# Stage four of a mixed-radix Fourier transform in quarters of the array, one pool of eight PSUM banks, and shorter rows

## The chip, the cores and the metric

The kernel runs on one NeuronCore of a Trainium2 chip. The metric is the device time in microseconds (us) of one launch, lower is better; the median of several runs counts. The engines are named as the profile names them: PE (TensorE, matmuls; PEld its weight loads), DVE (VectorE), ACT (ScalarE), POOL (GpSimd), SP (SyncE, which here only issues DMAs).

## The reference, cut to what matters

Eight sequences of 2496 tokens with 256 features are filtered along the sequence in frequency, and each token of the result then goes through one of eight experts.

```
X = np.fft.rfft(x, axis=1)                       # x: (8, 2496, 256)
Y = X * (filt_r + 1j * filt_i)[None]
y = np.fft.irfft(Y, n=2496, axis=1)
x = y.reshape(19968, 256)
logits = x @ w_gate                              # 8 experts
e = argmax(logits);  gate = softmax(logits)[e]
out = gate * (relu(x @ w1[e]) @ w2[e])           # w1: 256x1024, w2: 1024x256
```

Everything is in fp32.

## The kernel before, in words

**The transform.** 2496 is 39 x 64, so the transform over a sequence is one over 39 points (index q) for each of 64 residues t, and one over 64 points. A sequence goes through four stages, each a product with a table that lies in SBUF as the stationary operand.

- Stage one, `stage_a` (line 530): three residues t at a time, 3 x 39 = 117 rows by table `tas` give 3 x 2 x 20 = 120 rows (20 cosine and 20 sine coefficients for each residue; TP = 117, TK = 120, NB = 3). A residue group is a slot, there are NG = 22 of them, the last with one residue only. A chunk (`CH`) is four slots, or two at the end: 5 chunks of four and one of two in a batch.
- Stage two, `stage_b` (line 543): the 64-point transform on 128 rows, and the filter, four VectorE operations for each product.
- Stage three, `stage_c` (line 565): the 64-point transform back.
- Stage four, `stage_d` (line 580): back from 120 coefficients to 117 tokens with table `tds`. For each two slots of a chunk there is one product of 120 x 128 by 512 columns into a PSUM bank, which `evac` (line 410) copies to the tile `yo` on VectorE or ScalarE, whichever the planner has free first. In the last chunk the two slots have 120 and 40 rows and are two products of 256 columns.

Between stages one and two, and between three and four, a batch is written to DRAM (`zd`, `ud`) and read back in the other order; `by_part` (line 503) and `columns` (line 473) give the two orders. Batch 0 stays in SBUF instead (`first_a`, `turn_z`, `first_c`, `turn_u`).

**The routing.** `turn_y`, `block_logits` and `block_back` (lines 671 to 710) compute the logits of a chunk; from batch 3 on (`by_blocks`, line 690) the transpose is VectorE's. The logits' products go to 32 columns of the array each, four beside each other, into a PSUM bank of their own (`psr`, lines 697 and 718). `route` (line 739) finds the expert and the place of each token, writes the token's number and its gate into eight words each behind the 256 features of `yo` (rows of DR = 272 words, line 341), and scatters the rows to `rowsd` in DRAM, one indirect DMA on POOL for a slot, 22 a batch.

**The experts.** `rows_in` (line 949) reads the sorted rows of a tile of 512 (or 256, or 128) tokens; `hidden_by_quarters` (line 1020) and `hidden` compute the first product, `result` (line 1083) and, late in the kernel, `result_by_quarters` (line 1146) the second. The forms by quarters make seven block products out of eight, with sums on VectorE and POOL; that of the second product needs sums of the weights from POOL (`w2_sums`), and begins when the transforms are over (`late`).

**The order.** One loop at the end of the kernel writes all instructions. It plays the engines' clocks in a model (`Order`, line 125, with a cost for each instruction) and picks, step by step, either a transform step of the list that `slot` (line 1217) makes, or a step of one of the two streams of expert products; a step may be taken when its inputs and a PSUM bank (two for steps over 0.9 us of TensorE) are free in the model (`wait_of`). Each step is a tuple of due time, function, input it needs loaded, TensorE time by the model, stream, and what must be ready. Slot k holds stages two and three of batch k, stage one of batch k + 1 and stage four of batch k - 1. SBUF loads go out on SP in the order of the steps (`more_loads`), stores when their data is ready in the model (`move`, `flush`). PSUM has seven banks in one pool (line 354), of which `bank` (line 396) takes the one free first, and the eighth for the logits (line 359).

Of the kernel before, what the change touches and what calls it, by code (L numbers as in the profile page):

```python
# [19 lines left out]
P = 128  # L20
# [14 lines left out]
TK = NB * NS  # L35
DH = D // P
# [4 lines left out]
NJ = D // CT  # L41

# [13 lines left out]
def dft_tables():  # L56

    w = 2.0 * np.pi
    q = np.arange(N1)
    t = np.arange(N2)

    ta = np.zeros((NB, N1, NB, NS))
    td = np.zeros((NB, NS, NB, N1))
    for f in range(NF):
        ang = w * ((q * f) % N1) / N1
        for j in range(NB):  # L70
            ta[j, :, j, f] = np.cos(ang)
            td[j, f, j] = (2.0 if f else 1.0) / S * np.cos(ang)
            if f:
                ta[j, :, j, NF + f] = -np.sin(ang)
                td[j, NF + f, j] = -2.0 / S * np.sin(ang)

    ang = w * ((t[:, None] * t[None, :]) % N2) / N2
    c, sn = np.cos(ang), np.sin(ang)
    tb = np.block([[c, -sn], [sn, c]]).reshape(2, N2, P).transpose(1, 0, 2).reshape(P, P)
    tc = np.block([[c, sn], [-sn, c]]).reshape(P, 2, N2).transpose(0, 2, 1).reshape(P, P)  # L80

    ids = np.zeros((NB, N1, NG))
    valid = np.zeros((NB, N1, NG))
    for j in range(NB):
        for i in range(len(range(j, N2, NB))):
            ids[j, :, i] = token(q, NB * i + j)
            valid[j, :, i] = 1.0

    by_block = np.zeros((4, CT, NG + 2))
    by_block.reshape(P, NG + 2)[:TP, :NG] = valid.reshape(TP, NG)  # L90
    by_block = by_block.reshape(4, CT, -1, 4).transpose(3, 1, 2, 0).reshape(P, -1)

    sg = np.where(coefficients() <= S // 2, 1.0, -1.0)

    return {
        "ta": ta.reshape(TP, TK),
        "tb": tb,
        "tc": tc,
        "td": np.pad(td.reshape(TK, TP), ((0, 0), (0, P - TP))),
        "sg": np.concatenate([sg[:, :NF // 2], sg[:, NF // 2:]]),  # L100
        "ids": ids.reshape(TP, NG),
        "valid": np.concatenate([np.pad(valid.reshape(TP, NG), ((0, P - TP), (0, 0))), by_block], axis=1),
    }


def lay_x(x):

    out = np.zeros((x.shape[0], P, NG, D), x.dtype)
    q = np.arange(N1)
    for j in range(NB):  # L110
        for i in range(len(range(j, N2, NB))):
            out[:, j * N1:(j + 1) * N1, i] = x[:, token(q, NB * i + j)]
    return out
# [11 lines left out]
class Order:  # L125
# [53 lines left out]
    def count(self, engine, op, args, named):  # L179
# [31 lines left out]
        else:  # L211
            if out is None:
                took = 0.8 if engine == "sync" else 0.02
            elif engine == "tensor":
                if start > self.busy + 1.2:
                    self.slow = start + 3.4
                rows = out.ap[0][1]
                took = max(0.1, 0.00085 * n) if op == "transpose" else max(0.216, 0.00169 * n) if rows > 32 else 0.00045 * n
                took *= 2.0 if start < self.slow else 1.0
                tail = 0.25  # L220
            elif engine == "vector":
                took = 0.15 + n / 960
            elif engine == "scalar":
                took = 0.16 + n / 1200
            else:
                took = 0.2 + n / 480
# [24 lines left out]
class Slots:  # L251
# [3 lines left out]
    def freed(self, name, tag):  # L255

        if name is None:
            return 0.0
        if tag in self.live and name in self.live[tag]():
            return 1e9  # L260
        return max(self.order.done.get(name, 0.0), self.order.used.get(name, 0.0)) + 0.1
# [32 lines left out]
def kernel(  # L294
# [12 lines left out]
    ids: bass.AP,  # L307
    valid: bass.AP,
# [25 lines left out]
    TR = E * TE  # L334

    dram = open_pool(ctx, name="dram", bufs=1, space=DRAM)
    zd = [dram.tile([N2, NS, D], F32, tag=f"z{b % 2}", name="zd") for b in range(B)]
    ud = [dram.tile([N2, NS, D], F32, tag=f"u{b % 2}", name="ud") for b in range(B)]


    DR = D + 16
    rowsd = dram.tile([TR, DR], F32, tag="rows", name="rows")
# [11 lines left out]
    ps = open_pool(ctx, name="ps", bufs=7, space=PSUM)  # L354
# [4 lines left out]
    psr = open_pool(fft, name="psr", bufs=1, space=PSUM)  # L359

    tas = cst.tile([TP, TK], F32, name="tas")
    tbs = cst.tile([P, P], F32, name="tbs")
    tcs = cst.tile([P, P], F32, name="tcs")
    tds = cst.tile([TK, P], F32, name="tds")
# [15 lines left out]
    ids0 = cst.tile([TP, NG], F32, name="ids0")  # L380
    vld = cst.tile([P, 2 * NG + 2], F32, name="vld")
# [12 lines left out]
    ps.live["bank"] = lambda: ()  # L394
# [25 lines left out]
    def load_filters(c):  # L420
        f0, n = FH[c]
        if c == 0:
            nc.sync.dma_start(out=tbs, in_=tb)
# [11 lines left out]
        if c == 0:  # L435
            nc.sync.dma_start(out=tcs, in_=tcm)

    def load_rest():
        nc.sync.dma_start(out=tds, in_=td)
# [33 lines left out]
    def columns(ap, i0, n):  # L473

        rows = ap.rearrange("t s d -> (t s) d")
        m = min(n, NG - 1 - i0)
        yield TK, slice(0, m), rows[i0 * TK:(i0 + m) * TK, :].rearrange("(i p) d -> p i d", p=TK)
        if m < n:
            yield NS, slice(m, n), rows[(NG - 1) * TK:, :].rearrange("(i p) d -> p i d", p=NS)
# [23 lines left out]
    def by_part(ap):  # L503

        return ap.rearrange("t (c f) d -> (t c) f d", c=2)

# [8 lines left out]
    def load_z(b, c):  # L515
        f0, n = FH[c]
        zi = fin(("z", b, c))
        nc.sync.dma_start(out=zi[:, :n], in_=by_part(zd[b])[:, f0:f0 + n, :])

    def load_u(b, c):  # L520
        i0, n = CH[c]
        ui = fin(("u", b, c))
        for r, m, v in columns(ud[b], i0, n):
# [5 lines left out]

    def stage_a(b, c):  # L530
        i0, n = CH[c]
        xt = ins.pop(("x", b, c))
        zo = sb.tile([TK, 4, D], F32, tag="st", name="zo", bufs=4)
        for j in range(0, n, 2):
            p = bank()
            mm(p[:TK, :], lhsT=tas, rhs=xt[:TP, j:j + 2, :], start=True, stop=True)
            evac(zo[:, j:j + 2, :], p[:TK, :].rearrange("p (t d) -> p t d", t=2), 512)
        for r, m, v in columns(zd[b], i0, n):
# [4 lines left out]
    def stage_b(b, f):  # L543
# [6 lines left out]
        mm(p, lhsT=tbs, rhs=zi[:, j:j + 2, :], start=True, stop=True)  # L550
# [14 lines left out]
    def stage_c(b, f):  # L565
# [4 lines left out]
        uo = outs["u", b]  # L570
        p = bank()
        mm(p, lhsT=tcs, rhs=ys, start=True, stop=True)
        evac(uo[:, j:j + 2, :], p.rearrange("p (i d) -> p i d", i=2), 512)
        if j == 2:
            f0 = f - 2
            move(by_part(ud[b])[:, f0:f0 + 4, :], uo)
# [3 lines left out]
    def stage_d(b, c):  # L580
# [7 lines left out]
        yo = outs["o", b, c] = sb.tile([P, 4, DR], F32, tag="y", name="yo", bufs=YB)  # L588
        for j in range(0, n, 2):
            p = bank()  # L590
            if i0 + j + 2 < NG:
                mm(p, lhsT=tds, rhs=ui[:TK, j:j + 2, :], start=True, stop=True)
# [6 lines left out]


# [12 lines left out]
    def first_a(c):  # L613
        i0, n = CH[c]
        xt = ins.pop(("x", 0, c))
        for j in range(0, n, 2):
            p = bank()[:, :4 * TK]
            for h in range(DH):
                for i in range(2):
                    mm(p[:, (2 * h + i) * TK:(2 * h + i + 1) * TK], lhsT=xt[:TP, j + i, h * P:(h + 1) * P], rhs=tas,  # L620
# [21 lines left out]
    def first_c(f):  # L642
        ys = outs.pop(("y", 0, f))
        p = bank().rearrange("p (h i t c) -> p h i t c", h=DH, c=2, i=2)
        for i in range(2):
            for h in range(DH):
                mm(p[:, h, i].rearrange("p t c -> p (t c)"), lhsT=ys[:, i, h * P:(h + 1) * P],
                   rhs=tcs, start=True, stop=True)
# [44 lines left out]
    def block_logits(b, c):  # L693
# [3 lines left out]
        lt = psr.tile([P, 2, E * NG], F32, tag="lt", name="lt").rearrange("p i w -> p (i w)")[:, :n * CT]  # L697
# [14 lines left out]
    def logits(b, g):  # L712
# [5 lines left out]
        lt = psr.tile([P, 2, E * NG], F32, tag="lt", name="lt")[:, :, :TP]  # L718
# [20 lines left out]
    def route(b, c0, c1):  # L739
# [63 lines left out]
        if by_blocks(b):  # L803
# [13 lines left out]
            nc.vector.tensor_copy(row.rearrange("p (c g) -> p g c", g=4), pr[:, :, 0])  # L817
# [5 lines left out]
        for i, yo in enumerate(yos):  # L823
            n = min(4, w - 4 * i)
            sh8 = (TP, n, 8)
            nc.gpsimd.tensor_scalar(
                yo.bitcast(I32)[:TP, :n, D:D + 8], in0=ids0[:, t0 + 4 * i:t0 + 4 * i + n, None].to_broadcast(sh8),
# [3 lines left out]
        for i in range(w):  # L831
            m = N1 if t0 + i == NG - 1 else TP
            rows.append((row[:m, i:i + 1], yos[i // 4][:m, i % 4, :]))
        for i, (at, what) in enumerate(rows):
            m = what.ap[0][1]
            nc.gpsimd.tensor_copy(what[:, D + 8:], sd[:m, i:i + 1].to_broadcast((m, 8)))
# [7 lines left out]
    def pad_rows():  # L844
# [7 lines left out]
        nc.gpsimd.memset(fill.bitcast(I32)[:, D:D + 8], N)  # L852
# [96 lines left out]
    def rows_in(i):  # L949
# [4 lines left out]
        ng = gis[i] = pools["moe"].tile([P, 4, DR - D], F32, tag="ng", name="ng", bufs=8)  # L954
# [128 lines left out]
    def result(i, j):  # L1083
# [12 lines left out]
        gate = gis[i][:, j, 8:9]  # L1096
# [49 lines left out]
    def result_by_quarters(i):  # L1146
# [7 lines left out]
        gate = gis[i][:, :, 8:9]  # L1154
# [62 lines left out]
    def slot(k):  # L1217
# [12 lines left out]
        elif k < B:  # L1230
            for f in range(0, NF + 4, 2):
                at = f / (NF + 4)
                if f < NF:
                    steps.append((at, lambda f=f: stage_b(k, f), ("z", k, f // 4) if f % 4 == 0 else None, 0.85, "b", lambda f=f: count("y") < 4 and [ins["z", k, f // 4]]))
                if f >= 4:
                    steps.append((at + 0.01, lambda f=f: stage_c(k, f - 4), None, 0.85, "c", lambda f=f: [outs["y", k, f - 4], 0.0 if f % 4 else sb.free("st") - 0.9]))
        if k + 1 < B:
            for c in range(nch):
                steps.append(((0.25 if k == 0 else 0.0) + 0.7 * c / nch, lambda c=c: stage_a(k + 1, c), ("x", k + 1, c), 0.43 * CH[c][1], "a", lambda c=c: [ins["x", k + 1, c], sb.free("st") - 0.9]))
        if k > 0:  # L1240
            for c in range(nch + 3):
# [3 lines left out]
                if c < nch:  # L1245
                    steps.append((at, lambda c=c: stage_d(k - 1, c), ("u", k - 1, c) if k > 1 else "y", 0.43 * CH[c][1], "d",
                                  lambda c=c: [ins["u", k - 1, c] if k > 1 else outs["ui", c], sb.free("y") - 0.9]))
                if by_blocks(k - 1):
                    if 1 <= c <= nch:
                        steps.append((at + 0.03, lambda c=c: turn_y(k - 1, c - 1), None, 0.0, "d", lambda c=c: len(yts) < 2 and [outs["o", k - 1, c - 1]]))  # L1250
# [174 lines left out]
    def second_products():  # L1425

        for i in range(NT - RARE):
            if late and i < LARGE:
# [37 lines left out]
    with tc.manual_schedule(engines=None):  # L1466
        warm()
        nc.sync.dma_start(out=tas, in_=ta)
# [5 lines left out]
        def wait_of(f):  # L1474
# [11 lines left out]
            banks = ps.free("bank") if f[3] < 0.9 else max(ps.free("bank"), ps.free("bank", 1) - 0.85)  # L1486
# [15 lines left out]
        while fs or any(heads):  # L1502
# [7 lines left out]
            choice[0 if credit > 0.0 or not fs else 1:0] = products  # L1510
# [64 lines left out]
```

## Time and profile before

| what | us |
|---|---|
| median of three runs | 1476.66 (1476.07 to 1478.16) |
| the profiled execution | 1478.19 |
| its span on the core | 1476.5 |
| PE busy, records | 1440.1, 7828 |
| weight loads busy | 1147.0 |
| DVE busy | 848.7 |
| POOL busy | 822.0 |
| ACT busy | 480.6 |
| stage four of batch 3 begins, of batch 7 ends | 282, 879 |
| last scatter of rows begins | 959.8 |

A busy time is the sum of the times in which the engine had at least one instruction under way; matmuls overlap each other, so a record's mean length is longer than the time that it adds. A product in fp32 shows as two matmul records. The time before 970 us holds the transforms with expert products between them; what follows is expert products alone.

### The profile page before, as it was taken

To read this page: it belongs to the slowest core of one execution; us is meant where nothing else is said; L and a number is where in the kernel's file an instruction comes from. 1 tells how busy PE (TensorE), PEld (TensorE's weight loads), DVE (VectorE), ACT (ScalarE), POOL (GpSimd) and SP (SyncE) were. 2 spreads that over 40 slices of the span, in tenths; PEclk is the share of its full clock that TensorE was granted. 3 is DMA by queue.
4 is the path that set the end of the run, shared out by engine and by line. 5 is a ranking of instruction groups with operands and counts; after the bars stand their busy time and mean duration, and the time that the engine had idled before them with its cause. 6 is when DMAs were issued, how large, how long until landed. Compare 5 with 4: busy or idle time off the path is not lost.

```text
span 1476.5 us, 25693 instructions
## 1 busy us (share of the span) xinstructions
PE 1440.1 (98%) x7828; PEld 1147.0 (78%) x7828; DVE 848.7 (57%) x1819; ACT 480.6 (33%) x1004; POOL 822.0 (56%) x1213
## 2 busy tenths in 40 slices
PE   8998998999999999999999999999999999999998
PEld 6543656877677777776787778879999998999997
DVE  4667579235866675457665465567878775431110
ACT  4554452333332232322222232223232322223332
POOL 4434445635555654655465656858989878831111
PEclk9999999999999999999999999999999999999999
DMA  9759889795985585556544735556655425456661
GB/s 269 230 193 340 280 291 299 253 258 185 321 206 167 172 260 151 131 162 229 156 119 132 214 93 148 153 177 188 173 173 167 133 71 137 135 189 176 174 190 43
DMA packets 216383, 278.19 MB, mean 188 GB/s; under 512 B 124131, under 2 KB 163708, under 8 KB 216245
## 3 DMA queue, kind: packets, MB, share of 16 engines
q1 hardware_dynamic: 197125, 233.19, 53.2%
q0 software_dynamic: 19120, 43.33, 8.4%
q8 instruction: 66, 1.08, 0.3%
q14 instruction: 72, 0.59, 0.1%
HBM read 196.45 MB, written 80.64 MB: 188 GB/s over the span
## 4 chain that ended last, share of the span: by engine, by line
PE 85%; DVE 6%; DMA 4%; issue 3%; ACT 1%; POOL 0%; SPq 0%; DVEq 0%; POOLq 0%; ACTq 0%
PE bank L246 83%; DMA fin<-in_x_dram 2%; PE lt L246 2%; DVE hT L246 1%; DVE yw L246 1%; DVE ys L246 1%; DMA fin<-ud 1%; DMA fin<-zd 1%; DMA zd<-zo 1%; POOL out_dram L246 0%; DVE take L246 0%; ACT hT L246 0%; SPq L246 0%; DMA w1t<-in_moe_w_dram 0%; DMA xg<-rows 0%
## 5 line engine op out<-in xcount | busy, mean ns | idle before, releaser
L246 DVE TENSOR_TENSOR hT<-bank,hT 128x512 f32<-128x512 f32 (+1 forms) x504 | 301.9, 626 | 181.4 <-PE bank L246 101.2
L246 PE MATMUL bank<-w2t,hT 128*128 128x256 f32 (+1 forms) x1984 | 388.6, 350 | 1.6 <-DVE hT L246 1.6
L246 PEld LDWEIGHTS bank<-w2t,hT 128*128 128x128 f32 x1984 | 334.5, 190 | 49.9 <-issue 9.6
L246 PE MATMUL bank<-xT,w1t 128*128 128x256 f32 (+1 forms) x1728 | 314.9, 328 | 0.3 <-DVE hT L246 0.3
L246 POOL DMA_INDIRECT out_dram<-ys,ng x161 | 160.0, 994 | 252.5 <-ACT ys L246 121.5
L246 PEld LDWEIGHTS bank<-xT,w1t 128*128 128x128 f32 x1728 | 264.6, 191 | 33.1 <-issue 9.9
L246 ACT ACTIVATE hT<-hT 128x1024 f32<-128x1024 f32 (+1 forms) x144 | 135.5, 960 | 399.8 <-DVE hT L246 387.4
L246 POOL DMA_INDIRECT rows<-yo,row x176 | 181.9, 1033 | 70.8 <-POOL yo L246 31.3
L246 ACT ACTIVATE ys<-bank,ng 128x256 f32<-128x256 f32 x102 | 48.4, 475 | 287.4 <-PE bank L246 231.7
L246 PE MATMUL bank<-sums,wsum 128*128 128x256 f32 (+1 forms) x576 | 135.7, 358 | 1.5 <-DVE hT L246 1.5
L246 PE MATMUL bank<-w2s,hT 128*128 x592 | 132.9, 380 | 1.3 <-ACT hT L246 1.3
L246 POOL TENSOR_TENSOR wsum<-w1t 128x256 f32<-128x256 f32 x72 | 60.1, 835 | 114.5 <-PE bank L246 96.7
L246 PEld LDWEIGHTS bank<-w2s,hT 128*128 128x128 f32 x592 | 110.2, 190 | 15.8 <-ACT hT L246 2.0
L246 PEld LDWEIGHTS bank<-sums,wsum 128*128 128x128 f32 x576 | 100.3, 190 | 21.6 <-issue 11.3
L246 DVE STREAM_TRANSPOSE xT<-xg 128x512 f32<-128x512 f32 (+2 forms) x126 | 57.5, 494 | 57.7 <-PE bank L246 56.9
L246 PE MATMUL bank<-ys,tcs 128*128 128x512 f32 x140 | 73.8, 613 | 7.6 <-DVE yw L246 4.2
L246 DVE TENSOR_TENSOR ys<-bank,ht 128x512 f32<-128x512 f32 x80 | 54.9, 686 | 44.3 <-PE bank L246 38.0
L246 PE MATMUL bank<-fin,tds 120*128 120x512 f32 (+1 forms) x168 | 77.1, 580 | 3.1 <-DMA fin<-ud 2.6
L246 PE MATMUL bank<-fin,tas 117*120 117x512 f32 x154 | 75.5, 608 | 4.2 <-DMA fin<-in_x_dram 3.3
L246 PE MATMUL bank<-fin,tbs 128*128 128x512 f32 x140 | 72.7, 607 | 2.3 <-DMA fin<-zd 2.2
L246 ACT ACTIVATE hT<-bank 128x128 f32<-128x128 f32 (+1 forms) x191 | 57.2, 303 | 53.9 <-PE bank L246 45.3
L246 PE MATMUL bank<-xT,wsum 128*128 128x256 f32 (+1 forms) x288 | 68.8, 362 | 1.1 <-DVE yw L246 0.9
(171 smaller groups left out, 1778.9 us busy)
## 6 DMA issues: line engine op xcount, KB each, us to landing
w1t<-in_moe_w_dram SPq DMA_DIRECT2D x126, 512.0 KB
w2t<-in_moe_w_dram SPq DMA_DIRECT2D x68, 512.0 KB
fin<-in_x_dram SPq DMA_DIRECT2D x39, 512.0 KB
fin<-zd SPq DMA_DIRECT2D x35, 512.0 KB
ud<-uo SPq DMA_DIRECT2D x35, 512.0 KB
fin<-ud SPq DMA_DIRECT2D x35, 512.0 KB
zd<-zo SPq DMA_DIRECT2D x35, 480.0 KB
xg<-rows SPq DMA_DIRECT2D x112, 128.0 KB
```

Source lines behind the costliest of these rows:

```text
L246: return real(*args, **named)
```

## The change

- **The pool.** PSUM is one pool of eight banks; the logits take theirs from `bank` like all others. A bank that holds an unfinished half of stage four is kept from being given out.
- **Stage four in quarters, batches BD = 3 to 7.** The rows of a token group are arranged so that row r of one half stands for q and its partner for 39 - q. The cosine part of the coefficients gives the even half, the sine part the odd half, each 60 rows (of 64) by 60. A chunk becomes four products of 64 x 64 (two row halves by two column halves of the array) into two banks, one for cosine and one for sine; the sine bank is evacuated to `yo`, and `fold_y` on VectorE then makes the sum and the difference with the other bank. The same is written for stage one from batch BA on, with `fold_x`, and BA is 8. There are batches 0 to 7.
- **The tables.** `tas`, `tbs`, `tcs` and `tds` become one tile each, with a second version (permuted rows, or quarters) that `load_table` reads into the same tile during the slot before it is first needed (`tc` in slot 2, `td` in slot 3; `ta` and `tb` in slots 6 and 7).
- **The layout of `ud`** for batches 3 to 7 is 22 slots of 128 rows, of which 8 in each slot are padding, filled once for each of two buffers; a store of stage three is two DMAs, one of 126 partitions and one of 2.
- **The rows.** DR is 264 words (four for the token's number, four for the gate). From batch 3 on 124 rows of each slot are scattered; those that stand for no token go to waste rows behind the others.
- **The rest.** `ng` has seven buffers instead of eight. The late second product takes its quarter form only if the sums for that tile are begun or an earlier tile took it. The model prices a 64-row product at 0.29 us (0.17 for 256 columns), steps of no TensorE time ask for no bank, and those of stages one and four always for two.

```diff
+TH = NB * NF
+YR = 64 + TH
+BA, BD = 8, 3
...
-    zd = [dram.tile([N2, NS, D], F32, tag=f"z{b % 2}", name="zd") for b in range(B)]
-    ud = [dram.tile([N2, NS, D], F32, tag=f"u{b % 2}", name="ud") for b in range(B)]
-    DR = D + 16
+    zd = [dram.tile([NG * P, D], F32, tag=f"z{b % 2}", name="zd") for b in range(B)]
+    ud = [dram.tile([NG * P, D], F32, tag=f"u{b % 2}", name="ud") for b in range(B)]
+    ud[BD + 2:] = [ud[BD + b % 2] for b in range(B - BD - 2)]
+    DR = D + 8
...
-    ps = open_pool(ctx, name="ps", bufs=7, space=PSUM)
+    ps = open_pool(ctx, name="ps", bufs=8, space=PSUM)
...
+    def load_table(name, of, k):
+        tables[name] = cst.tile([P, P], F32, tag=name, name=name)
+        nc.sync.dma_start(out=tables[name], in_=of[k])
...
-    ps.live["bank"] = lambda: ()
+    ps.live["bank"] = lambda: {p.name for key, p in outs.items() if key[0] == "odd"}
...
+        if b >= BD:
+            m = n // 2
+            both = [bank() for _ in range(2)]
+            for h in range(2):
+                for part in range(2):
+                    k = slice(64 * part, 64 * part + TH)
+                    mm(both[part][64 * h:64 * h + 64, :m * D].rearrange("p (i d) -> p i d", i=m), lhsT=tds[k, :64],
+                       rhs=ui[k, h * m:(h + 1) * m, :], start=True, stop=True)
+            evac(yo[:, m:n, :D], both[1][:, :m * D].rearrange("p (i d) -> p i d", i=m), m * D)
+            outs["odd", b, c] = both[0]
+            return
...
+    def fold_y(b, c):
+        m = CH[c][1] // 2
+        even = outs.pop(("odd", b, c))[:, :m * D].rearrange("p (i d) -> p i d", i=m)
+        yo = outs["o", b, c]
+        nc.vector.tensor_tensor(yo[:, :m, :D], even, yo[:, m:2 * m, :D], op=ALU.add)
+        nc.vector.tensor_tensor(yo[:, m:2 * m, :D], even, yo[:, m:2 * m, :D], op=ALU.subtract)
...
-        lt = psr.tile([P, 2, E * NG], F32, tag="lt", name="lt").rearrange("p i w -> p (i w)")[:, :n * CT]
+        lt = bank()[:, :n * CT]
...
+        for name, of, when, at, where in (("ta", ta, BA - 2, 0.65, "a"), ("tb", tb, BA - 1, 0.76, "b"),
+                                          ("tc", tcm, BD - 1, 0.95, "c"), ("td", td, BD, 0.95, "d")):
+            if k == when:
+                steps.append((at, lambda name=name, of=of: load_table(name, of, 1), None, 0.0, where))
...
-            if late and i < LARGE:
+            if late and i < LARGE and (wide or i in made):
...
-            banks = ps.free("bank") if f[3] < 0.9 else max(ps.free("bank"), ps.free("bank", 1) - 0.85)
+            banks = 0.0 if not f[3] else ps.free("bank") if f[3] < 0.9 and f[4] not in "ad" else max(ps.free("bank"), ps.free("bank", 1) - 0.85)
```

## The prediction

> **What bounds the kernel now.** I read the page's busy table and chain first, then TensorE's groups with shapes kept apart, then the timeline around the products that the change touches, then one window over them.
>
> ```profile
> PE 1440.1 (98%) x7828; PEld 1147.0 (78%) x7828; DVE 848.7 (57%) x1819; ACT 480.6 (33%) x1004; POOL 822.0 (56%) x1213
> ...
> PE 85%; DVE 6%; DMA 4%; issue 3%; ACT 1%; POOL 0%; SPq 0%; DVEq 0%; POOLq 0%; ACTq 0%
> ```
>
> TensorE (PE) is busy 98% of the span, and 85% of the chain that ended last is its own matmuls. So a microsecond of matmul that disappears should shorten the span by nearly one, as long as the engine is fed. Stage four is `bank<-fin,tds`, in three shapes, one record for each half of an fp32 product:
>
> ```profile
> L246 PE MATMUL bank<-fin,tds 120*128 120x512 f32 x140 | 68.4, 614 | 3.1 <-DMA fin<-ud 2.6 <-ACT hT L246 0.4
> ...
> L246 PE MATMUL bank<-fin,tds 40*128 40x256 f32 x14 | 4.9, 428 | 0.0
> L246 PE MATMUL bank<-fin,tds 120*128 120x256 f32 x14 | 4.4, 394 | 0.0
> ```
>
> 140 records are 70 products over seven batches (batch 0 reads another tile), ten a batch, and two short pairs a batch. Means of one overlap their neighbours, so I price by the distance between starts. Columns: start, length, engine.
>
> ```profile
> 700.89 1.88 PE L246 MATMUL bank<-fin,tds 120*128 120x512 f32 x4
> 702.61 1.03 PE L246 MATMUL bank<-xT,wsum 128*128 128x256 f32 x4
> 703.48 7.07 PE L246 MATMUL bank<-w2t,hT 128*128 128x256 f32 x32
> 710.48 0.64 PE L246 MATMUL lt<-yt,wb 128*32 128x128 f32 x16
> 711.05 3.72 PE L246 MATMUL bank<-w2t,hT 128*128 128x256 f32 x16
> ...
> 639.30 1.28 PE L246 MATMUL bank<-fin,tds 120*128 120x256 f32 x4
> 640.51 1.78 PE L246 MATMUL bank<-xT,w1t 128*128 128x256 f32 x7
> ```
>
> A chunk of four slots holds TensorE from 700.89 to 702.61: 1.72 us, 0.43 for each of four records. The last chunk of a batch holds it from 639.30 to 640.51: 1.21 us. The engine's other neighbours in the time where the edited products lie (batches 3 to 7, 282 to 879 us):
>
> ```profile
> 282.00:879.00 597.00, 591.12 (x2902) 443.62 (x2900) 360.18 (x763) 186.45 (x368) 320.58 (x506) 1.00 0.63 189
> ```
>
> Columns: window, length, then busy PE, weight loads, DVE, ACT, POOL, and clock, DMA share, GB/s. PE is idle 5.9 us of 597; DVE (VectorE) is busy 60%, ACT (ScalarE) 31%, POOL 54%, DMA 63%. No second engine is near its limit.
>
> **What the Trainium skill says.** "TensorEngine Tiling (Array Packing)", Tiling Modes, Key Properties, says that tiles of the array load and multiply in parallel, and that a change of tiling mode drains the engine. The trace agrees for column tiles: the 16 records of `lt<-yt,wb` above, four column tiles wide, take 711.05 - 710.48 = 0.57 us. A 128-column record alone is half of a 256-column one ((710.48 - 703.48)/32 = 0.219), 0.11 us; sixteen in a row would be 1.75, four rounds of four side by side 0.44. So they do run side by side, at 0.13 us of entry and exit. Row tiles (two halves of the rows, as the change has too) are shown by no run yet. "PSUM — Partial Sum Buffer", section PSUM bank collisions, says that different row tiles may not write one bank at once; stage four takes two banks, one for each row half, which obeys that. The trace has no such pair.
>
> **The change, part by part.** BA is 8 and there are batches 0 to 7, so no batch meets `b >= BA`: stages one and two are computed as before, and `fold_x` never runs. BD is 3: only stages three (a permuted table) and four of batches 3 to 7 change. That is 5 batches of 5 full chunks and 1 short one.
>
> *The products.* A full chunk was two products over the array and becomes four over its quarters, 512 columns each. If the four run side by side it is one round of first halves and one of second halves, 2 x 0.43 = 0.86 us, and the switching. Low end for that: 0.13, as with `lt`. High end: the short chunk, four records of 256 columns, takes 1.21 where 4 x 0.215 = 0.86 would do; it has a 40-row product in it, so 0.35 is what it costs to go into a smaller row form and out. I take 0.29, near the high end, because the new group uses rows as well as columns: 1.15 us. Saved: 25 x (1.72 - 1.15) = 14.3 us. A short chunk becomes 2 x 0.215 + 0.29 = 0.72: 5 x (1.21 - 0.72) = 2.4. Together **16.7 us less TensorE**; with the ends, 25 x 0.73 + 5 x 0.65 = 21.5 and 25 x 0.51 + 5 x 0.43 = 14.9.
>
> *The fold.* Each chunk drops one of two evacuations and gains two DVE operations out of PSUM and SBUF.
>
> ```profile
> L246 DVE TENSOR_TENSOR hT<-bank,hT 128x512 f32<-128x512 f32 x392 | 257.8, 685 | 138.5 <-PE bank L246 92.6 <-ACT hT L246 30.9 <-issue 1.5
> ...
> L246 DVE TENSOR_TENSOR hT<-bank,hT 128x256 f32<-128x256 f32 x112 | 44.0, 421 | 42.9 <-ACT hT L246 29.1 <-PE bank L246 8.6
> ...
> L246 ACT COPY yo<-bank 128x512 f32<-128x512 f32 x82 | 47.8, 587 | 39.4 <-PE bank L246 29.5 <-issue 5.2 <-DMA rows<-yo,row 4.5
> ```
>
> At 685 and 421 ns it is 25 x 1.37 + 5 x 0.84 = 38.5 us more DVE; ACT loses about 30 copies, some 16 us. DVE goes from 360 of 597 us (60%) to about 399 of 584 (68%). Behind the fold on DVE's queue stand the sums of the experts' hidden layer and stage two's four operations; for them wait TensorE's banks and stage three. The even half's bank also stays taken until both folds are done, some 2 us more. What hides this is that TensorE takes other products (two expert streams, eight banks where seven were general), and that DVE at 79% between 1000 and 1100 us leaves PE idle for nothing there. I charge 3 us, an estimate: the 5.9 us of PE idle in the window times the growth of load over slack, (0.68/0.32)/(0.60/0.40) = 1.4, gives 2.4, and a little for the banks. Ends: 0, and, with all cover gone, 30 x 1.3 = 39.
>
> *The queues.* SP issues five more stores a batch (each `ud` store in two pieces, the second of two partitions), one `u` load less, two fills for each of two batches, four tables of 64 KB and one list: about 30 DMAs net. At 0.33 us for a `ud` store on SP's queue that is 10 us on a queue that mostly waits for buffers. A table load must wait until the old table's last product is done, and the expert weights queued behind it on SP wait too; the loads stand after those products in the order, so I charge 0 (bounds 0 and 2). The tables of stages one and two are loaded and never used. POOL issues the same 22 scatters a batch at 1.03 us, now of 124 rows, and copies 4 words for 8: 0. The waste rows are 5 x (22 x 124 - 2496) = 1160 rows of 1056 bytes, 1.2 MB of 278: 0. A row of 264 words for 272 is 3% fewer bytes of scatter, hidden either way: 0, bounds -1 and 1.
>
> *The pool and the rest.* The bank that only `lt` had joins the seven. In the stretch after the transforms PE already shows no idle (100.00 of 100 us from 1000 to 1100), so 0, with 2 us of gain as an end. `ng` in seven buffers for eight: rows are fetched at most two tiles ahead, so 0. The late expert products begin in the cheaper form only if their sums are begun: nine tiles use that form now (nine sums `hsum` of each kind in the groups), and one may fall back. It has 56 products of 128 columns for 32 of 256: 32 x 0.43 - 56 x 0.215 = 1.7 us lost if so; I charge 0.8.
>
> *Sum.* -16.7 + 3 + 0.8 = -12.9. The profiled execution took 1478.19 us, span 1476.5: it becomes 1465.3. It lies 1.5 us above the median of the runs, 1476.66, so the forecast for the median is **1464 us**.
>
> **Rivals.** *(A) The row halves do not run side by side, slower.* Place: each of the 30 groups. Only the pairs of columns overlap, so a full group is 4 x 0.43 + 0.35 = 2.07 us in place of 1.72 and a short one 4 x 0.215 + 0.35 = 1.21 as before: 25 x 0.35 = +8.8, with the 3 of the fold +12: 1489 us. It decides from 1.72 us for a group. For it: no row tiles in the trace, and the 40-row records lie 0.31 us apart where 256 columns take 0.215. Against it: four column tiles do overlap. *(B) DVE's queue takes the gain back.* If each of 30 groups costs PE 0.4 us of wait, 12 us stand in place of the 3: -16.7 + 12 + 0.8 = -3.9, 1473. For it: in the window DVE operations come in bursts, stage two's four at 0.69 us in a row. Against it: PE waited for DVE under 6 us in 597. *(C) Nearly free switching and use of the eighth bank:* 21.5 us less, 2 more, 1 back: 1454.
>
> **How the numbers follow.** Forecast 0.58, A 0.12, B 0.19, C 0.11. This kernel can be told from no change at about 0.2%, 3 us: faster is below 1473.7, slower above 1479.6. Forecast and C are faster; of B I count 0.10 faster, 0.07 the same and 0.02 slower; of the forecast 0.02 fall to the same. Faster 0.77, same 0.09, slower 0.14. The range is 1455 to 1476: it leaves out A, the worst of B, and half of C.
>
> **What would show it.** In the profile after: stage-four records of 64 by 64, eight to a group, and the next product 1.0 to 1.25 us after the first (1.72 or more is A); PE busy some 16 us lower; DVE about 38 us higher and ACT about 15 lower; PE's waits for DVE under 10 us between 282 and 879 (30 us of them would be B); the late expert products in the cheaper form for eight or nine tiles. The prediction is wrong if PE's idle time grows by more than its busy time falls.

## The result and the profile after

The changed kernel takes 1471.67 us (median of 22 runs) where the kernel before, measured beside it, takes 1477.99: a ratio of 0.9953 with a 95% interval of 0.9941 to 0.9964. That is 6.3 us by the medians and 7 by the ratio, half of the 12.9 that was forecast. The time lies inside the forecast range and on the forecast side.

The profiled execution took 1468.79 us (span 1467.1), 2.9 us less than the median. Two further profiles of the same program (`after_again` and E14 below) have spans of 1474.4 and 1472.4, so one span stands for some 4 us either way, and the verdicts below rest on ratios of timed runs. Here is the page's busy table and its line for the software DMA queue.

```profile
PE 1428.1 (97%) x7900; PEld 1133.4 (77%) x7900; DVE 869.7 (59%) x1869; ACT 461.0 (31%) x977; POOL 841.8 (57%) x1211
...
q0 software_dynamic: 28080, 44.03, 9.8%
```

TensorE is busy 12.0 us less than before (9.2 and 8.7 less in the two further profiles), and its idle time, span less busy, went from 36.4 us to 39.0 (43.5 and 41.0). VectorE (DVE) has 21 us more: the fold's 60 operations add 38, and other work there fell by 17. ScalarE (ACT) has 20 us less. POOL has 20 us more, for nearly as many instructions. The software queue, which carries the scatters, has 28080 packets for 19120, though hardly more bytes: that was not forecast.

**The products.** These are TensorE's groups by shape: stage four of the late batches, and the cheaper form of the late expert products.

```profile
L296 PE MATMUL bank<-fin,td 60*64 60x512 f32 x200 | 28.1, 613 | 0.2 <-DVE yw L296 0.2
...
L296 PE MATMUL bank<-tsum,hT 128*128 128x128 f32 x128 | 15.6, 275 | 0.0
L296 PE MATMUL bank<-fin,td 60*64 60x256 f32 x40 | 3.3, 402 | 0.0
```

The first and third lines are the quarters: 200 records are 25 full groups of eight, 40 are five short ones. The second line tells how many late tiles take the cheaper form, at 16 records a tile: eight, where the kernel before had nine. A mean of 613 ns says nothing of the price, since the four quarters lie over one another (200 of 613 ns would be 123 us; the group is busy for 28.1). Starts do say it. In TensorE's timeline the columns are start, length, engine, what, and how many records.

```profile
402.84 0.59 PE L296 MATMUL bank<-xT,w1t 128*128 128x256 f32 x2
403.36 1.09 PE L296 MATMUL bank<-fin,td 60*64 60x512 f32 x8
404.38 1.13 PE L296 MATMUL bank<-sums,wsum 128*128 128x256 f32 x4
405.35 1.03 PE L296 MATMUL bank<-xT,w1t 128*128 128x256 f32 x4
```

From the group's first start to the next product is 404.38 - 403.36 = 1.02 us. The two expert records ahead should take 2 x 0.215 = 0.43 and take 0.52, and the four behind it should take 0.86 and take 0.97. So a group costs 1.02 + 0.09 + 0.11 = 1.22 us. The short one, in the same columns:

```profile
471.29 0.81 PE L296 MATMUL bank<-xT,w1t 128*128 128x256 f32 x3
472.04 0.66 PE L296 MATMUL bank<-fin,td 60*64 60x256 f32 x8
472.63 1.13 PE L296 MATMUL bank<-sums,wsum 128*128 128x256 f32 x4
```

It costs 0.59 + 0.2 = 0.79. The old short chunk also had 0.11 behind it, 1.32 in all. Saved: 25 x (1.72 - 1.22) + 5 x (1.32 - 0.79) = 15.2 us.

**The window of batches 3 to 7**, with the columns of the forecast's own line (busy PE, weight loads, DVE, ACT, POOL, clock, DMA share, GB/s):

```profile
282.00:879.00 597.00, 586.82 (x3060) 439.62 (x3058) 405.00 (x858) 168.88 (x346) 360.37 (x527) 0.99 0.66 191
```

DVE is at 68%, as forecast, and PE's idle time there rose from 5.9 to 10.2 us. POOL has 360 us for 321. The waits of TensorE in that window (us in all, times, longest) say what the 10.2 us are. Kernel after:

```profile
PE bank L296 <- DMA w2t<-in_moe_w_dram: 4.1, 1, 4.1
PE bank L296 <- DVE hT L296: 2.0, 3, 1.0
PE bank L296 <- ACT hT L296: 1.3, 4, 0.4
PE bank L296 <- DVE yw L296: 1.2, 2, 1.0
PE bank L296 <- DVE yt L296: 0.8, 2, 0.6
```

Kernel before:

```profile
PE bank L246 <- DVE ys L246: 1.1, 1, 1.1
PE lt L246 <- DVE yt L246: 1.0, 1, 1.0
PE bank L246 <- DVE yw L246: 0.9, 1, 0.9
PE bank L246 <- ACT hT L246: 0.9, 2, 0.4
PE bank L246 <- DVE ls L246: 0.8, 1, 0.8
```

With the smaller ones, the waits for DVE are 4.2 us after and 4.4 before: they did not grow. The largest wait after is a single one, for an expert's weights, which the change doesn't touch.

**Where that wait comes from.** The next lines are the scatters `rows<-yo,row` (least, median and greatest ns of one; first and last start). Kernel before:

```profile
L246 POOL DMA_INDIRECT rows<-yo,row x176: 917/1006/1472, 86.0 to 959.8; - x176
```

Kernel after:

```profile
L296 POOL DMA_INDIRECT rows<-yo,row x176: 913/1335/1707, 88.0 to 971.7; - x176
```

A scatter of 124 rows takes POOL 1.34 us where one of 117 took 1.01. SP's read of the rows waits until the scatters issued so far have landed. Of batch 3 these are the first eight, which start on POOL from 316.3 to 330.9 us; at 0.33 us each they take 2.7 us more. SP's timeline in the kernel after shows what stands behind that read:

```profile
327.24 0.38 SPq L296 DMA_DIRECT2D w1t<-in_moe_w_dram  x1
335.95 2.14 SPq L296 DMA_DIRECT2D xg<-rows  x4
338.14 0.39 SPq L296 DMA_DIRECT2D ng<-rows  x1
338.64 0.92 SPq L296 DMA_DIRECT2D fin<-zd  x2
339.65 1.33 SPq L296 DMA_DIRECT2D ud<-uo  x2
342.44 3.25 SPq L296 DMA_DIRECT2D w2t<-in_moe_w_dram  x2
```

SP's own waits between 325 and 352 us put 7.4 us to one wait for these rows:

```profile
SPq L296 <- DMA rows<-yo,row: 7.4, 1, 7.4
```

Next come, in order, the rows and their gates, two transform loads, two stores, and only at 342.44 the second-layer weights `w2t`. TensorE runs out of work on the way:

```profile
340.78 3.72 PE L296 MATMUL bank<-xT,w1t 128*128 128x256 f32 x16
348.64 6.35 PE L296 MATMUL bank<-w2t,hT 128*128 128x256 f32 x16 [4.14 <-DMA w2t<-in_moe_w_dram]
```

It waits 4.14 us, and then sixteen records take 6.35 us that take 3.62 elsewhere in this case, because the granted clock is lower: the window from 340 to 360 us has a clock of 0.83.

```profile
340.00:360.00 20.00, 15.86 (x76) 11.46 (x75) 6.24 (x12) 4.24 (x12) 11.34 (x16) 0.83 0.62 203
```

The Trainium skill ("TensorE: Matmul & The Clock Gate", Part 1) says that an idle window of about 3.4 us puts TensorE at half its clock until a busy one has passed. The trace agrees: 4.14 us of waiting bring 6.35 - 3.62 = 2.7 us more, so that the wait costs 6.9. The two further profiles have the wait at the same instruction, 3.7 and 4.7 us long.

**A second wait, ahead of the window.** At 258 us TensorE waits for a load of `zd`, the input of stage two:

```profile
258.39 2.00 PE L296 MATMUL bank<-fin,tb 128*128 128x512 f32 x2 [4.71 <-DMA fin<-zd]
```

In SP's queue two things that the change adds stand ahead of that load, the second table of stage four (`td`) and the two fills of the padding (`ud<-ht`):

```profile
239.19 0.80 SPq L296 DMA_DIRECT2D td<-in_td_dram  x1
240.04 2.80 SPq L296 DMA_DIRECT2D fin<-in_x_dram  x1
242.94 0.39 SPq L296 DMA_DIRECT2D zd<-zo  x1
243.38 2.83 SPq L296 DMA_DIRECT2D ud<-ht  x2
246.25 3.82 SPq L296 DMA_DIRECT2D fin<-ud  x2
250.17 0.55 SPq L296 DMA_DIRECT2D fin<-zd  x1
```

The two further profiles have this wait too (5.9 and 4.9 us), and so have those with scatters of 128 rows (4.5, 3.9 and 6.1). The kernel before has no such wait there; at 239 us it waits 3.4 us for DVE. In a profile of the same order with more DVE work (E8 below) the wait for `zd` is absent, though the queue is the same. No run takes the table or the fills away with the order held, so what they cost stays open.

### The profile page after: what moved, and what is told of

It is laid out like the page before. It is cut to its first block, busy times and chain, and to the rows that moved or that the text cites. A ratio compares the mean times of both kernels' runs of the same rounds, so it can differ in the third digit from the quotient of the medians.

```text
span 1467.1 us, 25910 instructions
## 1 busy us (share of the span) xinstructions
PE 1428.1 (97%) x7900; PEld 1133.4 (77%) x7900; DVE 869.7 (59%) x1869; ACT 461.0 (31%) x977; POOL 841.8 (57%) x1211
## 3 DMA queue, kind: packets, MB, share of 16 engines
q0 software_dynamic: 28080, 44.03, 9.8%
## 5 line engine op out<-in xcount | busy, mean ns | idle before, releaser
L296 PE MATMUL bank<-w2t,hT 128*128 128x256 f32 (+1 forms) x1984 | 397.8, 355 | 5.7 <-DMA w2t<-in_moe_w_dram 4.1
L296 PEld LDWEIGHTS bank<-w2t,hT 128*128 128x128 f32 x1984 | 341.6, 192 | 62.6 <-issue 14.2
L296 POOL DMA_INDIRECT rows<-yo,row x176 | 218.1, 1239 | 75.7 <-POOL yo L296 46.7
L296 POOL TENSOR_TENSOR wsum<-w1t 128x256 f32<-128x256 f32 x72 | 57.1, 793 | 108.6 <-PE bank L296 70.6
L296 PE MATMUL bank<-fin,tb 128*128 128x512 f32 x140 | 73.8, 616 | 6.7 <-DMA fin<-zd 6.5
L296 PE MATMUL bank<-fin,ta 117*120 117x512 f32 x154 | 75.0, 606 | 3.6 <-DMA fin<-in_x_dram 3.5
L296 PE MATMUL bank<-ys,tc 128*128 128x512 f32 x140 | 73.3, 609 | 2.7 <-DVE ys L296 1.7
L296 PE MATMUL bank<-sums,w1t 128*128 128x256 f32 (+1 forms) x288 | 67.4, 357 | 0.3 <-DVE yo L296 0.2
```

Of the source, the lines that this page charges most:

```text
L296: return real(*args, **named)
```

## The experiments

Each ratio is to the kernel before on the same chip, with its 95% interval. The recorded expectations call the runs E1 to E17; the labels stand beside the results. One matter governs how they may be read. The kernel's order of work comes from a planner that prices every step, so almost any edit rewrites the order of all engines. Where the text says "same order", the edit was made so that TensorE, DVE, ACT and SP have the same instructions in the same order as the kernel it is compared with, apart from the edited ones.

### The scatters of 124 rows

Theory: they are slow by their row count, and cost time through SP's queue. Rival: the extra bytes and the waste rows cost it, or nothing does. The edit scatters all 128 rows of a slot (the four more go to waste rows); same order.

```diff
-            m, at = (TP, ids0) if b < BD else (YR, lids[:YR])
+            m, at = (TP, ids0) if b < BD else (P, lids)
...
-            m = YR if b >= BD else N1 if t0 + i == NG - 1 else TP
+            m = P if b >= BD else N1 if t0 + i == NG - 1 else TP
```

> The changed kernel with all 128 rows of a slot scattered in batches 3 to 7 in place of 124 (the four further rows go to waste rows that are there already); order of every engine but POOL is the same. In the changed kernel a scatter of 124 rows takes 1.35 us on POOL, one of 117 rows took 1.01, one of 128 rows takes 0.98. Theory (row count): 124 is a number that POOL splits badly, and with 128 a scatter is back at 1.0 us, POOL is about 37 us less busy and the small packets of 16 bytes are gone. If POOL or the scatters' DMA are what holds back the gain, the time falls by 3 to 6 us against the changed kernel (ratio to before 0.991 to 0.993); if they lie beside the matmuls, the time stays at 0.9953 within 0.1%. Rival (waste rows): the waste rows themselves cost, then a scatter takes 1.35 us or more here too.

> E2 once more, to narrow its interval: the changed kernel with 128 rows for 124 in the scatters, same order. In E2's profile the wait of 4.1 us for w2 at 345 us and the half clock behind it are gone. If that is what the longer scatters cost, the time is 3 to 7 us below the changed kernel (0.990 to 0.993), if something else is late next it is 0.994.

> E2 a third time, beside E14: scatters of 128 rows, same order. Theory (scatters): 3 to 6 us below E14, wait near 345 us of about 1 us and full clock there. Rival: equal to E14 within 0.1%, and the differences of the earlier calls were between chips.

> The changed kernel as it is, on the same chip and in the same call as E15: the pair decides on the scatters. Ratio to before 0.994 to 0.996. Theory (scatters): it is 0.2% to 0.4% above E15, and its profile has the wait for w2 near 345 us of 3.5 us or more with half clock behind it.

> The changed kernel as it is, for a second profile and as the partner of the three above on one chip: ratio 0.9953 within its interval. Theory (order): the waits for DMA before 400 us that the first profile after shows (4.7 us for z at 254, 4.1 us for w2 at 345) stand in this profile too, at the same instructions. Rival: they are chance of that execution and lie elsewhere here.

Measured: 0.9930 (0.9907 to 0.9953) in E2, 0.9918 (0.9902 to 0.9934) in its repetition (E2b) and 0.9913 (0.9896 to 0.9931) in E15. The changed kernel unedited gave 0.9940 (0.9920 to 0.9960) beside E2 (`after_again`) and 0.9949 (0.9936 to 0.9962) beside E15 (E14). In the second pair the two intervals lie apart; the medians are 1466.19 and 1470.19 us. The first pair alone would not have told them apart. The scatters of the 128-row kernel:

```profile
L296 POOL DMA_INDIRECT rows<-yo,row x176: 917/999/1492, 90.8 to 972.8; - x176
```

More rows, less time. Its software queue:

```profile
q0 software_dynamic: 17520, 44.34, 8.4%
```

So 110 scatters of 124 rows had 28080 - 17520 = 10560 packets more than 110 of 128, 96 a scatter; the trace has them as packets of 16 and 12 bytes. SP's wait for the rows falls there from 7.4 us (8.3 in E14) to 2.9:

```profile
SPq L296 <- DMA rows<-yo,row: 2.9, 1, 2.9
```

At the place where the changed kernel waited, TensorE hardly does:

```profile
349.75 3.72 PE L296 MATMUL bank<-xT,w1t 128*128 128x256 f32 x16
353.90 2.40 PE L296 MATMUL bank<-w2t,hT 128*128 128x256 f32 x10 [0.43 <-DMA w2t<-in_moe_w_dram]
```

It waits 0.43 us for the same weights. What follows: the row count costs some 4 us (4.0 by the medians of E14 and E15, 0.9949 - 0.9913 = 0.36% or 5.3 by their ratios; 3.1 and 1.5 in the first pair), without a single product changed. The bytes went up and the time down, which excludes the rival.

### Everything but the quarters

> The changed kernel with BD = 8: stage four stays whole in all batches, there is no fold, no second tables, no waste rows; the pool of eight banks, the rows of 264 words, the seven ng buffers and the changed bank rules stay. Theory (order): the quarters themselves save their 13 to 15 us, and what is missing of the forecast comes from the rest of the change, which gives another order of steps and with it waits for DMA before 400 us; then this kernel is 3 to 8 us slower than before (ratio 1.002 to 1.005). Rival (fold): the rest is free, the folds on DVE and the quarters' own side effects eat half of the gain; then this kernel equals the one before within 0.1%.

```diff
-BA, BD = 8, 3
+BA, BD = 8, 8
```

With this, no batch uses quarters; the new tables, the fold and the waste rows go too, and the one pool and the short rows stay. Measured (E1): 1.0029 (1.0015 to 1.0044), as the theory had it, beside the changed kernel's 0.9940. The quarters with all that comes with them are worth 0.9%, 13 us, between these two orders. But this kernel is slower than the one before although nothing in it should be. Its TensorE timeline has, ahead of a stage-four product, a wait that the kernel before doesn't have:

```profile
263.01 3.75 PE L296 MATMUL bank<-fin,td 120*128 120x512 f32 x4 [8.81 <-DMA fin<-ud]
```

SP's waits from 240 to 262 us show the same path as above, with scatters of 117 rows:

```profile
SPq L296 <- DMA rows<-yo,row: 9.4, 1, 9.4
```

In this order the load that TensorE needs stands behind the read of the rows, so a long scatter isn't needed for that path to cost time. That raised the question whether the pool or the rows cost something, and the next experiments took each alone.

### The rows of 264 words alone

> The kernel before with rows of 264 words alone. Theory (rows): rows of 1056 bytes cost DMA, and this kernel is 3 to 5 us slower than before, with longer packets of rows in the trace. Rival (order): the packets take as long as before (256-byte reads 21 to 24 ns, four rows in one packet of the scatter), and the time lies within 5 us of before on either side, by its waits.

> The kernel before with rows of 264 words, as E7, but the planner's model is told the sizes of rows of 272, so that the order of all engines is exactly that of before. Theory (order): E7's 0.5% was another order, the shorter rows themselves cost nothing, and this kernel equals before within 0.15%. Rival (rows): rows of 1056 bytes cost DMA or POOL time that the packets do not show, and this kernel is 5 to 9 us slower than before (1.0035 to 1.006).

```diff
-    DR = D + 16
+    DR = D + 8
```

In the kernel before, this edit alone (E7) gives 1.0050 (1.0030 to 1.0070), slower. In the second version (E9) the planner is still told the old sizes, so that the order is that of the kernel before: 1.0005 (0.9990 to 1.0019). The rows cost nothing that can be told from noise; the order that they led to cost 0.5%. Its new wait stands in the waits of TensorE between 700 and 720 us:

```profile
PE bank L246 <- ACT uo L246: 3.8, 1, 3.8
```

> The changed kernel with all 128 rows of a slot scattered (as E2) and rows of 272 words as before (eight words each for number and gate). The scatters are back at 1.0 us, and the 4 us wait for w2 at 345 us should be gone as in E2. Theory (order): another order, the time lies within 5 us of E2. Rival (rows): it is 5 us or more faster than E2 (ratio to before 0.989).

The changed kernel with 128-row scatters and rows of 272 words (E11) gives 0.9925 (0.9909 to 0.9940), beside 0.9918 with 264 (E2b): no difference, though the order is another one.

### The pool

> The kernel before with the pool of eight banks alone (the logits take theirs from it). Theory (pool): 3 to 5 us slower than before, as E1. Rival (order): within 5 us of before on either side, with idle time of PE between 100 and 400 us that goes with it[...].

> The changed kernel with the logits' bank given back: seven banks in the pool, one for the logits alone. E1 showed that the change without its quarters is 0.29% (4 us) slower than before. Theory (pool): the shared eighth bank is what costs it, then this kernel is 3 to 5 us faster than the changed one (ratio to before 0.991). Rival (order): no single part costs it, each part only gives the planner another order with other waits for DMA before 400 us; then this one lies anywhere within 5 us of the changed kernel, and its waits stand at other places or are other waits.

```diff
-    ps = open_pool(ctx, name="ps", bufs=7, space=PSUM)
+    ps = open_pool(ctx, name="ps", bufs=8, space=PSUM)
...
-        lt = psr.tile([P, 2, E * NG], F32, tag="lt", name="lt").rearrange("p i w -> p (i w)")[:, :n * CT]
+        lt = bank()[:, :n * CT]
```

The kernel before with this alone (E6) gives 0.9930 (0.9913 to 0.9947), more than the whole change. The reverse, seven banks and one in the changed kernel (E5), gives 1.0022 (1.0010 to 1.0034), a loss of 0.7%. In both, theory and rival missed: each kernel lies some 10 us from the one it was edited from, in the direction opposite to the theory. Both have new orders. So the same was asked of the order by itself.

### The order by itself

A constant of the planner, `HOP`, is its estimate of how long a result takes from engine to engine. It changes the order, and through it which engine takes a copy and how many late tiles take the cheap form: nine in E10 and E13 as in the kernel before, eight in E12 for nine in E6, ten in E17 for eight in E15.

> The kernel before with one constant of the planner's model moved (the hop between two engines 0.12 us in place of 0.10): the same work on every engine, another order of it. Theory (order): the time moves by 2 to 8 us in either direction, with the idle time of PE, as much as E6 and E7 moved it. Rival: a new order is worth under 2 us, and E6 and E7 were the pool and the rows.

> The kernel before with the hop at 0.08, a second order of it (E10 was one with 0.12, ratio 1.0003). Theory (order): an order alone moves the time by some 0.3% to 0.5%, as E7 (1.005) did although its rows cost nothing (E9); here either side. Rival: within 0.1% of before, and E7 was an outlier.

> E6 (before with the pool of eight alone) with the model's hop at 0.12 in place of 0.10, so a second order with the shared pool. Theory (pool): the eighth bank is worth 0.5% to 0.8% in any order, ratio to before 0.992 to 0.996. Rival (order): E6 had a lucky order, and this one lies within 0.3% of before.

> E15 (the changed kernel with scatters of 128 rows) with the model's hop at 0.12: a second order of it. Orders alone have moved the kernel before by 0.03% and 0.42%, and E6 by 0.84%. Theory (order): it lies within 0.8% of E15's 0.9913 to 0.993, more likely above. Rival: within 0.1%, the quarters leave the order less to decide.

```diff
-    HOP = 0.1
+    HOP = 0.12
```

In the kernel before: 1.0003 (0.9987 to 1.0020) at 0.12 (E10, as its rival had it) and 1.0042 (1.0029 to 1.0055) at 0.08 (E13). In the kernel before with the one pool, at 0.12 (E12, again as the rival had it): 1.0014 (1.0000 to 1.0028), where it had 0.9930 at 0.1. In the changed kernel with 128-row scatters, at 0.12 (E17): 0.9948 (0.9921 to 0.9975), where it had 0.9913 to 0.9930. So with the same products an order alone moved the time by up to 0.4% (E13) or 0.5% (E7 beside E9). Between E6 and E12 it is 0.8%, 12 us, of which the lost cheap tile is 1.7 by the forecast's price: nearly as much as the whole forecast. The pool's 0.7% is not shown to be the pool's: one other order takes it away. That it is worth nothing isn't shown either.

### The fold

> The changed kernel with the first operation of each fold written twice (same result): 30 more DVE operations of 0.685 us or 0.42, about 19 us of DVE between 283 and 877 us. Theory (order): DVE lies beside TensorE, the time changes by under 2 us. Rival (fold): the two fold operations, 38.5 us of DVE, cost TensorE about 6 us, so half as much again costs 3 us or more (ratio to before 0.9975 or higher).

> The changed kernel with the first operation of each fold written three times, the two further ones unseen by the planner's model, so that the order of work stays that of the changed kernel: 60 more DVE operations, 38.5 us more DVE between 283 and 877 us, as much as the folds themselves. Theory (hidden): the folds cost TensorE 3 us or less, and so do these: ratio to before 0.994 to 0.996. Rival (fold): E4, 0.41% slower than the changed kernel for half as much DVE, was DVE and not another order; then this one is 8 us or more slower than the changed kernel (0.9995 or more).

> The changed kernel without the second operation of each fold (the difference), which the planner's model still counts, so that the order stays: 30 DVE operations, 19 us, fewer. It leaves out the second half of the tokens' values in batches 3 to 7: they keep the odd part alone, and those tokens may go to other experts; the tiles and their sizes stay. E8 showed that 38.5 us more DVE in the same order cost 11 us, 0.29 us a microsecond. If the folds that are there cost as much, this kernel is 5.5 us faster than the changed one (ratio to before 0.991). If the cost grows with load (60%, 68%, 73% busy), the folds cost little and it is 0 to 2 us faster (0.9935 to 0.995).

```diff
         nc.vector.tensor_tensor(yo[:, :m, :D], even, yo[:, m:2 * m, :D], op=ALU.add)
+        for _ in range(2):
+            nc.nc.vector.tensor_tensor(yo[:, :m, :D], even, yo[:, m:2 * m, :D], op=ALU.add)
```

The first version (E4) wrote the fold's first operation twice with the planner's knowledge: 0.9981 (0.9967 to 0.9995), but in another order, so it settles nothing. The second (E8), above, hides two repetitions from the planner: same order, 60 operations or 38.5 us more DVE, 1.0016 (1.0003 to 1.0029). Against the changed kernel's 0.9953 that is 0.63%, 9 us (11 against its 0.9940): the theory, that they hide, is refuted for these. TensorE's waits from 282 to 879 us in that kernel:

```profile
PE bank L296 <- DVE yt L296: 6.2, 7, 2.0
PE bank L296 <- DMA w2t<-in_moe_w_dram: 3.7, 1, 3.7
PE bank L296 <- DVE hT L296: 3.3, 5, 1.0
```

Its DVE is at 72% in the window (431.85 of 597):

```profile
282.00:879.00 597.00, 577.02 (x2998) 429.60 (x2997) 431.85 (x903) 165.72 (x343) 349.25 (x509) 0.99 0.65 189
```

The waits for DVE are several short ones; they add up to 13.2 us, where the changed kernel has 4.2, so the difference is about the time lost. The third version (E16) leaves out the fold's second operation (so half of the token values of batches 3 to 7 are not formed, and tokens may go to other experts), while the planner still counts it; same order: 0.9924 (0.9898 to 0.9950). Against 0.9953 half the fold would be worth 0.3%, 4 us, with 0 to 8 by that interval. In its trace the waits for DVE are 3.0 us in that window, 1.2 fewer than in the changed kernel, which speaks for the low end. The fold's price lies between nothing and some 8 us or more, and the next 38.5 us after it cost 9 to 11. That is as near as these runs come.

### The best version

It is the changed kernel with scatters of 128 rows, 0.9913 to 0.9930 in three comparisons (0.9948 in the other order, E17), faster than both kernels; it is the first experiment's edit.

## Why the prediction was half right

**What bounds, and the products: right.** The row halves do run side by side: 1.02 us for a full group, which disproves rival A (it began at 1.72). The charge for switching was 0.29 us beside 0.86; it is 1.22 - 0.86 = 0.36, so 15.2 us in place of 16.7. TensorE's busy time fell by 9 to 12 us and not by the 13.5 that are left with the cheap tile below; half clock behind waits adds to it, as the 2.7 us above do. Rival C, nearly free switching, falls with that.

**The queues: the step that failed.** The prediction said that POOL "issues the same 22 scatters a batch at 1.03 us, now of 124 rows, and copies 4 words for 8: 0". It took a price from scatters of 117 rows for those of 124, and gave no bound. The price was 1.34. On POOL, busy 60% of the window, that might still have been hidden; it was not, because SP waits for scatters at the head of a queue that also carries expert weights. In place of 0 the term is some +4 us. The prediction named that queue, but only for the table loads, which it charged 0 with the fills. These stand ahead of the wait for `zd`; whether they bring it about isn't shown.

**The late expert product: mis-sized.** Eight tiles use the cheap form, not nine (128 records for 144, at 16 a tile). The full 1.7 us are due where 0.8 was charged; that price is the forecast's, no run measures it by itself. The edited condition alone does not lose the tile: with it in place E4 and E11 have nine such tiles and E17 ten. It is the order that decides.

**The fold: right in kind, its size unsettled.** DVE's load came out as forecast (68%), and so did the waits for DVE (4 us where under 10 were expected), so rival B isn't in the trace of this kernel. Nor is the growth of these waits from which the 3 us were worked out: they were 4.4 us before. But the slope is real: 38.5 us more cost 9 to 11. The 3 us are neither confirmed nor refuted.

**The pool and the rows: 0 with ends of 2 and 1 us was too narrow.** Not because they cost something by themselves (the rows do not, and of the pool it stays open), but because the order that an edit leads to is worth several tenths of a per cent by itself, 0.8% in one pair. The prediction had no term for it.

**The sum.** Products -15.2, cheap tile +1.7, scatters +4: -9.5, beside the measured -6.3 to -7. Some 3 us are left, as much as the fold was charged, but that agreement shows nothing. The fold may be 0 to 8, and the new order, with the wait for `zd` in it, is an unknown term of several us of either sign; only their sum is fixed by the rest, and no run here parts them. What is shown with unchanged order is the scatters, and with them mended the gain is 0.7 to 0.9%, the size of the forecast, in this one order.

## What to carry to other kernels

Price a step that is moved or resized by its new shape, and where no row of the trace has that shape, put a bound on it: seven more rows made a scatter a third dearer, and four more still made it cheap again. Follow a step that ends later to the in-order queue that waits for it, and read what else stands behind that wait; it was unrelated weights that came late here. When a planner orders the work, first measure what other orders of the same work give, and don't credit an edit with less than that, unless it was measured with the order held.

## What the hardware did that was not expected

- An indirect scatter takes 1.01 us with 117 rows, 1.34 with 124 and 0.99 with 128, and with 124 it has 96 packets more than with 128. The Trainium skill ("DMA: Bandwidth & Descriptors", Why a DMA increments its semaphore by 16 and not by 1) says that a transfer is spread over the largest number of DMA engines, up to 16, that divides the slowest dimension on both of its sides. That would be 16 for 128, 13 for 117, and 4 for 124, and fits the order of these times. The packet sizes in the traces agree. In the kernel before, 168 scatters of 117 rows left 2184 packets of one row, 13 each: 13 shares of nine rows, cut into packets of four, four and one. In the kernel after, 110 scatters of 124 rows left four packets of three rows each: four shares of 31. No run shows which engine took a share, and the only other count here is 39 rows, at 0.92 us.
- Four 64 x 64 quarters in fp32 run at once: 1.02 us for eight records of 512 columns, 0.59 for eight of 256, with 0.09 us ahead and 0.11 behind. Two groups in a row, at 277.95 us, hold TensorE for 1.88, less than twice 1.02, so part of the price falls once. The skill's page on tiling, named in the prediction, has the overlap; this is its price here.
- A long wait brought half clock without exception here. In the profiles of both kernels and of all versions, after the first 10 us, each of the 41 waits of TensorE of 3.44 us or more had half clock in it or right behind it, for 3.4, 6.8 or 10.2 us. Of shorter waits some had it and some not: one of 3.2 us for the same weights (E16) left the clock at 1.00.
